# Taking the weight splitting off GpSimd: low parts on VectorE, high parts on ScalarE, from the last routing of a routed mixture-of-experts layer on

## The chip, the cores and the metric

The kernel runs on one core of a Trainium2 chip. The metric is the device time of one execution in microseconds (us). Engines are called as the profile calls them: PE (TensorE, matrix products), DVE (VectorE), ACT (ScalarE), POOL (GpSimd) and SP (SyncE, which issues most transfers). Each engine works through its own instructions in the order of the program; semaphores tie the engines together.

## The reference

Three stages follow each other: attention with rotary embedding, a dense mixture of four experts on all tokens, and a routed layer of eight experts in which each token goes to one expert. The last two stages, cut to their core:

```python
# dense: x [1152, 512], w1 [4, 512, 1024], w2 [4, 1024, 512]
for e in range(E):
    h = np.maximum(x @ w1[e], 0.0)
    out += p[:, e:e + 1] * (h @ w2[e])

# routed: 8 experts of the same size
logits = xn @ en.T / tau
expert_idx = np.argmax(logits, axis=1)
gate_w = probs[np.arange(N), expert_idx]
for e in range(E):
    mask = expert_idx == e
    h = np.maximum(x[mask] @ w1[e], 0.0)
    out[mask] = gate_w[mask, None] * (h @ w2[e])
```

Inputs and outputs are float32.

## The kernel before

**Precision.** PE multiplies in float32r. To keep float32 accuracy every operand is held as a high part and a low part, hi + lo, and a product is three matmuls: hi·hi, hi·lo, lo·hi. So all weights have to be split on the chip. A weight unit is a [128, 2048] piece of an expert's weights: units 0 and 1 are halves of w1, 2 and 3 halves of w2. It is loaded into `raw[u]` and split into `wh[u]` and `wl[u]` in four pieces j of [128, 512]: a copy makes the high part (`wh`), a subtraction raw - wh makes the low part (`wl`). There is one buffer of each kind per unit.

**Where the pieces are split.** In the dense layer ACT copies (L657) and DVE subtracts (L658). From the last routing on, POOL takes a share. For the first block of the routed layer `first_split` sends the low part to POOL unless the piece is named in `FIRST_ON_DVE`: 6 pieces on DVE, 10 on POOL. For all later blocks `split_piece` sends piece j = 3 of each unit to POOL, and for the odd units 1 and 3 the high part of that piece to DVE (L655) instead of ACT:

```python
def split_piece(self, u, j):
    self.split_rows(u, j, *([self.nc.gpsimd, self.nc.vector if u % 2 else None] if j == 3 else []))
```

**The last routing.** Tokens come in nine chunks of 128. Chunks 0 to 5 are routed together; the last three (6, 7, 8) are routed one by one by `route_one` as their sums of the dense layer end. The steps of one chunk are, in order: `finish` (x1 from the sums, L814, and its sum of squares, L894, both DVE; then the root on POOL, `norm`, L905 and L906), `turn` (PE transposes x1, ACT copies to `xt`, L889), up to three steps of weight splitting, `pick` (PE logits, L900; DVE maximum `lm`, one-hot `oh`, reciprocal of the root L1082, `nb` L1084; ACT exponential `ex`, L1085), the other steps of splitting, and `slots` (PE ranks, L919 to L921; DVE slot numbers and gate, L1090 to L1095). `scatter` (L928, an indirect transfer issued by POOL) sends x1 to its expert's rows. The products of the sums run on PE between these steps (L804 to L806). After chunk 8 DVE makes a table of blocks (`block_table`), whose last part SP reads for the control of the loads.

**The routed layer.** 14 blocks of 128 tokens are always there (`SURE`); three more are conditional. For block b, `fc1(b, u)` is 12 matmuls (L1291, tile psa) with unit u, `relu` an ACT activation (L1315, h), `turn_h` four PE transposes (L1268), an ACT copy `hth` (L1269) and a DVE subtraction `htl` (L1270); `turn_x` does the same for the input (`bxh`, `bxl`); `fc2(b, u)` is 12 matmuls (tile pso) with unit 2 + u. In `block(b)` the order on PE is: turn_x(b+1), fc1(b, 1), turn_h(b, 0), fc1(b+1, 0), turn_h(b, 1), fc2(b, 0), fc2(b, 1). Every block splits all four units, and one unit's four pieces are put out beside each of these four groups of 12 matmuls: unit 3 of b beside fc1(b, 1), unit 1 of b+1 beside fc1(b+1, 0), unit 0 of b+2 beside fc2(b, 0), unit 2 of b+1 beside fc2(b, 1). `finish` scales the result on ACT (L1326) and scatters it to the output (L1327, issued by POOL). The order of everything from the dense layer on is the order of the code; no planner moves it.

Of the kernel before, what the change touches and what calls it, by code (L numbers as in the profile page):

```python
# [28 lines left out]
class Schedule:  # L29
    """Puts operations of several engines in order: a greedy run over estimated costs, in which  # L30
    a free engine takes the operation of the lowest rank among those that can start by then."""
# [7 lines left out]
    def op(self, rank, eng, cost, f, *a, after=(), slot=None, late=0.0):  # L39
        """slot names a buffer of a ring, held from the first operation that names it until all  # L40
        in self.free[slot] are over; late is what the result takes beyond the engine's time."""
        o = dict(rank=rank, eng=eng, cost=cost, f=f, a=a, after=list(after), slot=slot, late=late, end=None)
        self.ops.append(o)
        return o

    def start(self, o, now):
        """When an operation can start, None as long as that is open."""
        ends = [now[o["eng"]], o["ready"]]
        if o["slot"]:
            used, n = self.used[o["slot"][0]], self.rings[o["slot"][0]]  # L50
            if o["slot"] not in used and len(used) >= n:
                for e in self.free[used[-n]]:
                    if e["end"] is None:
                        return None
                    ends.append(e["end"] + self.RELEASE)
        return max(ends)
# [5 lines left out]
    def run(self):  # L62
        """The operations, as dicts, by their start."""
# [32 lines left out]
class Attention:  # L96
    """RoPE attention, two heads at a time; x^T goes to xh + xl (both float32r).

    Round r runs the scores and the softmax of pair r beside the transposes and the
    products with v of pair r - 1, and prepares the operands of pair r + 1.  # L100
    """
# [36 lines left out]
    # engines of the operations that have a choice, pair by pair  # L138
# [58 lines left out]
    def rope(self, eng, i, j, sl=slice(0, 2), cols=slice(0, S)):  # L197
        """Step j of x * cos + swapped x * sin, in place; slot 0 is q, 1 is k."""
        raw = self.st[i]["raw"]
        x, y = raw[:, sl, cols], raw[:, slice(sl.start + 2, sl.stop + 2), cols]  # L200
        if j < 2:
            z = (x, y)[j]
            self.by(eng).tensor_tensor(out=z, in0=z, in1=self.rope_t[:, j, sl, cols], op=ALU.mult)
        else:
            self.by(eng).tensor_tensor(out=x, in0=x, in1=y, op=ALU.add)
# [11 lines left out]
    def spread(self, i):  # L217
        """qa = [qh; ql] of head A, qb = [ql; qh] of head B, ka and kb = k of a head on both halves."""
        nc, st, A, B = self.nc, self.st[i], self.A, self.B
        n = st["n"]  # L220
        ka = st["ka"] = self.p_k.tile([128, 2, S], F32R, name="ka")
        kb = st["kb"] = self.p_k.tile([128, 2, S], F32R, name="kb")
        qa, qb = st["qa"], st["qb"] = self.qa[i % 2], self.qb[i % 2]
        dma = lambda out, in_: nc.sync.dma_start(out=out.bitcast(F32), in_=in_.bitcast(F32))  # L224
        dma(out=ka[A], in_=n[A, 1:4:2])
        dma(out=ka[B], in_=n[A, 1:4:2])
        dma(out=qa[A, 0:S], in_=n[A, 0])
        dma(out=qa[B, 0:S], in_=n[A, 2])
        dma(out=kb[A], in_=n[B, 1:4:2])
        dma(out=kb[B], in_=n[B, 1:4:2])  # L230
        for o, m, f in ((0, 512, 0), (S, 64, 512)):
            dma(out=qb[A, o:o + m], in_=n[B, 2, f:f + m])
            dma(out=qb[B, o:o + m], in_=n[B, 0, f:f + m])

    def first_pair(self, D):
        """Loads and operands of pair 0, in small parts and without DMAs between partitions;
        what each chunk of its scores waits for."""
# [73 lines left out]
    def qk(self, i, c):  # L311
        """Scores of row chunk c; chunks 0-3 head A, 4 the rests of both, 5-8 head B."""
# [100 lines left out]
    def av(self, i, h, hf, k):  # L413
        """One of the five key chunks of x^T; any of them may come first."""
# [11 lines left out]
    def av_shift(self, i, h, hf):  # L426
        """The low half of x^T moves to the rows of the main half."""
# [51 lines left out]
    def plan(self, last_round):  # L479
        """All operations, with what they wait for."""  # L480
# [14 lines left out]
        for i in range(NPAIR):  # L495
            # operands
# [34 lines left out]
            # scores and softmax  # L531
# [15 lines left out]
            # transposes and products with v  # L547
# [57 lines left out]
class Experts:  # L605
    """Both expert layers. A weight unit is [128, 2048]: 0 and 1 are the halves of w1's columns
    as [p, k, 512], 2 and 3 the halves of w2's rows as [p, f, 512]; each is held as hi + lo."""
# [6 lines left out]
    FIRST_ON_DVE = (0, 0), (0, 1), (2, 0), (2, 1), (2, 2), (3, 0)  # L614
# [6 lines left out]
    def open_right(self, ctx):  # L621
        """Weights and the first split unit, in place of what the attention no longer needs."""
# [28 lines left out]
    def split(self, cut, u, lo_eng=None, hi_eng=None):  # L651
        nc = self.nc
        raw, hi, lo = cut(self.raw[u]), cut(self.wh[u]), cut(self.wl[u])
        if hi_eng:
            hi_eng.tensor_copy(hi, raw)  # L655
        else:
            nc.scalar.activation(out=hi, in_=raw, func=AF.Copy)  # L657
        (lo_eng or nc.vector).tensor_tensor(out=lo, in0=raw, in1=hi.bitcast(F32), op=ALU.subtract)  # L658

    def split_rows(self, u, j, *engines):  # L660
        self.split(lambda t: t[:, j * 512:(j + 1) * 512], u, *engines)

    def split_cols(self, u, j, *engines):
        self.split(lambda t: t.rearrange("p (a b) -> p a b", b=512)[:, :, j * 128:(j + 1) * 128], u, *engines)

# [18 lines left out]
    def layer1(self, xh, xl, rest):  # L684
        """All but the routing of the last token chunk, which is left in self.todo."""
        tc = self.tc
        with ExitStack() as c1:
# [28 lines left out]
            for c in range(3):  # L716
# [9 lines left out]
                # the first block's weights are split beside the chunk's routing  # L726
# [8 lines left out]
    def first_split(self, u, *js):  # L735
        for j in js:
            self.split_rows(u, j, *[] if (u, j) in self.FIRST_ON_DVE else [self.nc.gpsimd])

# [5 lines left out]
    def next_splits(self, n):  # L744
        """Splits of the weights needed next; a unit's next load follows its split."""
# [71 lines left out]

    def router_setup(self):
# [30 lines left out]
        def scale():  # L849
            """Embeddings over tau (|emb| + 1e-6)."""  # L850
# [11 lines left out]
        def empty():  # L862
            """Empty slots: zero rows whose token lies beyond the output."""
# [15 lines left out]
    def turn(self, c, cols, ps=None):  # L879
        """Part of a chunk's x1^T."""  # L880
# [27 lines left out]
    def counts(self, c, ps=None):  # L908
        """Tokens per expert in the chunks before c, in every partition."""
# [4 lines left out]
    def rank(self, cs):  # L914
        """Slots: the expert's region + tokens before in the chunk + tokens of the chunks before."""
# [8 lines left out]
    def scatter(self, c):  # L924
        # no order among the scatters can be declared between direct neighbours on the engine
# [7 lines left out]
    def route(self, chunks):  # L933
        """Logits and the one-hot of the first largest."""
# [7 lines left out]
        # the sums of the last token block leave half of the accumulators free  # L942
# [34 lines left out]
    def first_block(self):  # L977
        """The expert with the most tokens in the first six chunks comes first, the others follow in turn, and
        the slots of its first block are filled (or left empty) by these chunks alone, so that the second layer
        can start with that block. Then slots and gates of these chunks."""  # L980
# [5 lines left out]
        def choose():  # L986
# [8 lines left out]
            # e1 = the first expert, place = (e - e1) mod 8  # L995
# [9 lines left out]
            # 128 rows of NT / 128 place  # L1005
# [5 lines left out]
            # later tokens of the first expert start at slot 128  # L1011
# [36 lines left out]
    def first_loads(self, *units):  # L1048
        """The first expert's weights."""
# [4 lines left out]
    def route_one(self, c, acc, between):  # L1054
        """The whole routing of one chunk, from the last expert's sum on."""
# [45 lines left out]
    def apart(self, inst, group):  # L1101
        """Scatters to rows of their own need no order among themselves."""
# [4 lines left out]
    def block_table(self):  # L1107
        """For the blocks of the sorted tokens: whether the expert is new, its first unit, the first slot, and
        whether the block is there at all."""
# [5 lines left out]
        def rows():  # L1115
# [18 lines left out]
            # first slot: 128 j + sum over finished experts of (region - 128 blocks)  # L1134
# [116 lines left out]
    def split_with(self, b, u):  # L1251
        """The split of a unit, in pieces that go with the products that follow."""
# [4 lines left out]
    def split_piece(self, u, j):  # L1257
        self.split_rows(u, j, *([self.nc.gpsimd, self.nc.vector if u % 2 else None] if j == 3 else []))
# [29 lines left out]
    def three(self, acc, ah, al, u, first, last, mid=None, mid_at=1, low_last=False):  # L1288
        """acc += a^T w over the unit's four row chunks, without the product of the two low parts."""
# [43 lines left out]
def constants(nc, p):  # L1333
# [21 lines left out]
    # routing: strictly earlier rows, and tables over experts and blocks  # L1355
# [60 lines left out]
def rope_tables():  # L1416
    """cos and signed sin by (row d, table, position)."""
# [8 lines left out]
def weight_units(w1, w2):  # L1426
    """Per expert four contiguous units [128, 2048]: halves of w1's columns, halves of w2's rows."""
# [35 lines left out]
```

## Time and profile before

| | |
|---|---|
| median of 3 runs | 804.32 us (803.84 to 804.36) |
| span of the profiled execution | 802.5 us; the runs lie some 1.8 us above it |
| busy: PE, DVE, ACT, POOL | 749.2, 490.5, 377.1, 252.7 us |
| L658, low parts | DVE 222 pieces, 190.1 us; POOL 62 pieces, 105.2 us |
| L657, high parts on ACT | 258 pieces, 143.1 us |
| L655, high parts on DVE | 26 pieces, 10.8 us |
| mean granted clock of PE | 0.989 of 2.4 GHz |

The span is measured from the first to the last instruction; the time of a run lies around it. A busy time is the sum over an engine's instructions, so an instruction that stands still inside its own span also counts as busy. A start-to-start distance of two neighbours on an engine (here called pitch) is what an instruction costs the engine's queue; its own duration can be longer, because the end of one overlaps the start of the next.

The last routing lies at 582 to 618 us of the span, the first blocks at 618 to 644, and from 646.82 on ten rounds follow that look alike.

### The profile page before, as it was taken

The numbers are of one execution on the slowest core, as the hardware profiler recorded it, in microseconds if no ns is written. First come the engines' busy times: TensorE is split into PE (matmuls) and PEld (weight loads), VectorE is DVE, ScalarE is ACT, GpSimd is POOL, SyncE is SP. The second block draws the span as 40 slices with busy tenths as digits, with TensorE's granted clock in tenths as the row PEclk, the third lists the DMA queues.
The fourth block names the chain that finished last, engine by engine and source line by source line (L and its number), as shares of the span: only waits on it lengthen the run. The fifth ranks groups of instructions, "written<-read, shape, count | busy, mean of one in ns | idle before, by whom it ended". The sixth has DMA issues, their size and how long they took to land.

```text
span 802.5 us, 11114 instructions
## 1 busy us (share of the span) xinstructions
PE 749.2 (93%) x4002; PEld 653.4 (81%) x4002; DVE 490.5 (61%) x840; ACT 377.1 (47%) x767; POOL 252.7 (31%) x180
## 2 busy tenths in 40 slices
PE   2798888999999999999999999999988799999996
PEld 1687777889999999999999999999966577777775
DVE  7889999997122351222512225232558999999994
ACT  5587888884101231112311123111234788788883
POOL 4777685223100000000000000000084567665662
PEclk9899999999999999999999999999997999999999
DMA  6766664534340089900390000000071265594010
GB/s 200 218 168 162 170 162 89 142 131 185 139 124 0 1 239 313 288 1 1 130 291 0 1 1 1 0 1 1 21 292 43 93 230 206 187 376 155 27 41 17
DMA packets 31837, 97.27 MB, mean 121 GB/s; under 512 B 4638, under 2 KB 6174, under 8 KB 25760
## 3 DMA queue, kind: packets, MB, share of 16 engines
q1 hardware_dynamic: 29936, 91.77, 36.6%
q0 software_dynamic: 1840, 4.73, 1.6%
q8 instruction: 33, 0.54, 0.3%
q14 instruction: 28, 0.23, 0.1%
HBM read 58.32 MB, written 27.09 MB: 106 GB/s over the span
## 4 chain that ended last, share of the span: by engine, by line
PE 58%; DVE 23%; issue 7%; ACT 5%; POOL 3%; SPq 2%; DMA 2%; ACTq 0%; POOLq 0%; DVEq 0%
DVE wl L658 12%; PE ps L788 8%; PE ps L790 8%; PE ps L789 8%; PE acc L806 8%; PE acc L804 8%; PE acc L805 8%; PE av L424 2%; PE sc L327 2%; DVE nm L337 2%; SPq L224 2%; PE psa L1291 1%; ACT wh L657 1%; DVE p L411 1%; ACT e L344 1%
## 5 line engine op out<-in xcount | busy, mean ns | idle before, releaser
L794 DVE SCALAR_TENSOR_TENSOR hl<-ps,hh 128x384 fp32r<-128x384 f32 x96 | 53.5, 558 | 269.6 <-ACT hh L793 269.6
L658 DVE TENSOR_TENSOR wl<-raw,wh 128x512 fp32r<-128x512 f32 x222 | 190.1, 897 | 4.7 <-ACT wh L657 4.7
L793 ACT ACTIVATE hh<-ps 128x384 fp32r<-128x384 f32 x96 | 47.1, 491 | 304.5 <-PE ps L790 302.9
L657 ACT ACTIVATE wh<-raw 128x512 fp32r<-128x512 f32 x258 | 143.1, 627 | 5.2 <-DMA raw<-in_w_dram 2.8
L788 PE MATMUL ps<-xh,wh 128*128 128x384 f32 x384 | 130.3, 339 | 0.0
L790 PE MATMUL ps<-xh,wl 128*128 128x384 f32 x384 | 129.7, 338 | 0.0
L789 PE MATMUL ps<-xl,wh 128*128 128x384 f32 x384 | 129.5, 337 | 0.0
L658 POOL TENSOR_TENSOR wl<-raw,wh 128x512 fp32r<-128x512 f32 x62 | 105.2, 1714 | 49.4 <-DVE wh L655 27.3
L905 POOL TENSOR_TENSOR ss<-ss,half 128x1 f32<-128x1 f32 (+1 forms) x5 | 3.5, 704 | 355.1 <-DVE sq L894 355.1
L806 PE MATMUL acc<-wh,hl 128*128 128x512 f32 x288 | 114.4, 397 | 0.0
L804 PE MATMUL acc<-wh,hh 128*128 128x512 f32 x288 | 114.4, 397 | 0.0
L805 PE MATMUL acc<-wl,hh 128*128 128x512 f32 x288 | 113.7, 395 | 0.0
L789 PEld LDWEIGHTS ps<-xl,wh 128*128 128x128 f32 x384 | 72.2, 188 | 3.9
L788 PEld LDWEIGHTS ps<-xh,wh 128*128 128x128 f32 x384 | 72.2, 188 | 3.8
L790 PEld LDWEIGHTS ps<-xh,wl 128*128 128x128 f32 x384 | 72.1, 188 | 0.0
L806 PEld LDWEIGHTS acc<-wh,hl 128*128 128x128 f32 x288 | 54.2, 188 | 12.5
L805 PEld LDWEIGHTS acc<-wl,hh 128*128 128x128 f32 x288 | 54.2, 188 | 8.8
L804 PEld LDWEIGHTS acc<-wh,hh 128*128 128x128 f32 x288 | 54.1, 188 | 8.3
L344 ACT ACTIVATE e<-sc,nm 128x576 f32<-128x576 f32 x72 | 53.4, 742 | 9.7 <-DVE nm L337 9.4
L337 DVE TENSOR_REDUCE nm<-sc 128x1 f32<-128x576 f32 x72 | 53.8, 750 | 2.8 <-PE sc L327 1.7
L389 PE MATMUL pt<-ident,e 128*128 128x128 f32 (+1 forms) x304 | 47.6, 283 | 7.4 <-DVE ptl L411 6.3
L1291 PE MATMUL pso<-wh,htl 128*128 128x512 f32 x112 | 44.6, 407 | 5.0 <-DVE htl L1270 5.0
(233 smaller groups left out, 1298.9 us busy)
## 6 DMA issues: line engine op xcount, KB each, us to landing
raw<-in_w_dram SPq DMA_DIRECT2D x40, 1024.0 KB, 5.6
xs<-z SPq DMA_DIRECT2D x10, 2056.0 KB, 14.3
raw<-in_qk_dram SPq DMA_DIRECT2D x7, 1152.0 KB, 5.3
ka<-n SPq DMA_DIRECT2D x14, 288.0 KB, 3.9
kb<-n SPq DMA_DIRECT2D x14, 288.0 KB, 4.4
xin<-xs SPq DMA_DIRECT2D x13, 257.0 KB, 4.0
rv<-in_v_dram SPq DMA_DIRECT2D x8, 320.0 KB, 5.4
qa<-n SPq DMA_DIRECT2D x14, 144.0 KB, 4.2
```

Source lines behind the costliest of these rows:

```text
L337: nc.vector.tensor_reduce(out=st["nm"][:, c:c + 1], in_=st["sc", c][:, :, :SH], axis=AX.XY, op=ALU.max, negate=True)
L344: nc.scalar.activation(out=e.rearrange("p (a b) -> p a b", a=2), in_=st.pop(("sc", c))[:, :, :SH], func=AF.Exp, bias=st["nm"][:, c:c + 1], ...
L657: nc.scalar.activation(out=hi, in_=raw, func=AF.Copy)
L658: (lo_eng or nc.vector).tensor_tensor(out=lo, in0=raw, in1=hi.bitcast(F32), op=ALU.subtract)
L788: nc.tensor.matmul(o, wcut(self.wh[u], k), xh[:, k, cs], start=(k == 0), stop=False)
L789: nc.tensor.matmul(o, wcut(self.wh[u], k), xl[:, k, cs], start=False, stop=False)
L790: nc.tensor.matmul(o, wcut(self.wl[u], k), xh[:, k, cs], start=False, stop=(k == 3))
L794: nc.vector.scalar_tensor_tensor(out=hl, in0=o, scalar=0.0, in1=hh.bitcast(F32), op0=ALU.max, op1=ALU.subtract)
L804: nc.tensor.matmul(acc, hh[:, js], wh, start=(f == 0), stop=False)
L805: nc.tensor.matmul(acc, hh[:, js], wl, start=False, stop=False)
L806: nc.tensor.matmul(acc, hl[:, js], wh, start=False, stop=(f == 7))
L1291: self.nc.tensor.matmul(acc, a[:, k * 128:(k + 1) * 128], w[u][:, k * 512:(k + 1) * 512], start=start, stop=stop)
```

## The change

From the last routing on, every piece is split as in the dense layer: ACT copies the high part and DVE subtracts the low part. `FIRST_ON_DVE` and the choice of engines go. 62 subtractions move from POOL to DVE (10 in the routing, 52 in the blocks), and 26 copies from DVE to ACT. Nothing is computed otherwise. The rest of the diff takes out comments and docstrings, four code lines less in all, so a line of the kernel after has a number four lower than before from `first_split` on (L658 is L654).

```diff
-    FIRST_ON_DVE = (0, 0), (0, 1), (2, 0), (2, 1), (2, 2), (3, 0)
...
-    def split(self, cut, u, lo_eng=None, hi_eng=None):
+    def split(self, cut, u):
         nc = self.nc
         raw, hi, lo = cut(self.raw[u]), cut(self.wh[u]), cut(self.wl[u])
-        if hi_eng:
-            hi_eng.tensor_copy(hi, raw)
-        else:
-            nc.scalar.activation(out=hi, in_=raw, func=AF.Copy)
-        (lo_eng or nc.vector).tensor_tensor(out=lo, in0=raw, in1=hi.bitcast(F32), op=ALU.subtract)
+        nc.scalar.activation(out=hi, in_=raw, func=AF.Copy)
+        nc.vector.tensor_tensor(out=lo, in0=raw, in1=hi.bitcast(F32), op=ALU.subtract)
...
     def first_split(self, u, *js):
         for j in js:
-            self.split_rows(u, j, *[] if (u, j) in self.FIRST_ON_DVE else [self.nc.gpsimd])
+            self.split_rows(u, j)
...
     def split_piece(self, u, j):
-        self.split_rows(u, j, *([self.nc.gpsimd, self.nc.vector if u % 2 else None] if j == 3 else []))
+        self.split_rows(u, j)
```

The first place is DVE's queue in the routing of chunk 6, from `nb` of its `pick` to chunk 7's `finish` (acc_5137 holds chunk 7's sums; raw_2067, wh_2218 and wl_2219 are unit 1). Before:

```order
L1084 TENSOR_SCALAR nb<-lm_5169,ss 128x1
L1090 SCALAR_TENSOR_TENSOR rk_5198,sl_5199<-ps,oh 128x8
L1092 CAST slot<-sl_5199 128x1
L1093 TENSOR_SCALAR es_5178<-es_5178 128x1
L1094 RECIPROCAL x_2072<-es_5178 128x1
L1095 TENSOR_TENSOR seen<-seen,oh 128x8
L814 SCALAR_TENSOR_TENSOR x_2072<-acc_5137,p,x_2072 128x256 x2
L894 SCALAR_TENSOR_TENSOR sq,ss<-x_2072 128x512
L1077 TENSOR_REDUCE lm_5251<-ps 128x1
```

And in the changed kernel:

```order
L1080 TENSOR_SCALAR nb<-lm_5169,ss 128x1
L654 TENSOR_TENSOR wl_2219<-raw_2067,wh_2218 128x512 x3
L1086 SCALAR_TENSOR_TENSOR rk_5198,sl_5199<-ps,oh 128x8
L1088 CAST slot<-sl_5199 128x1
L1089 TENSOR_SCALAR es_5178<-es_5178 128x1
L1090 RECIPROCAL x_2072<-es_5178 128x1
L1091 TENSOR_TENSOR seen<-seen,oh 128x8
L810 SCALAR_TENSOR_TENSOR x_2072<-acc_5137,p,x_2072 128x256 x2
L890 SCALAR_TENSOR_TENSOR sq,ss<-x_2072 128x512
L654 TENSOR_TENSOR wl_2219<-raw_2067,wh_2218 128x512
L1073 TENSOR_REDUCE lm_5251<-ps 128x1
```

Three subtractions of unit 1 now stand between chunk 6's `nb` and its slots, ahead of chunk 7's `finish`, and a fourth ahead of chunk 7's `pick`; before, POOL had them.

The second place is DVE's queue in one of the later blocks, from `bxl` to the next `bxl` (units by their tiles: wl_2223 is unit 3, wl_2219 unit 1, wl_2071 unit 0, wl_2221 unit 2). Before:

```order
L1270 TENSOR_TENSOR bxl<-ps,bxh 128x512
L1280 CAST btok<-xin 128x1
L658 TENSOR_TENSOR wl_2223<-raw_2069,wh_2222 128x512
L655 CAST wh_2222<-raw_2069 128x512
L658 TENSOR_TENSOR wl_2223<-raw_2069,wh_2222 128x512 x2
L1270 TENSOR_TENSOR htl_5843<-ps,hth_5842 128x512
...
L658 TENSOR_TENSOR wl_2219<-raw_2067,wh_2218 128x512
L655 CAST wh_2218<-raw_2067 128x512
L658 TENSOR_TENSOR wl_2219<-raw_2067,wh_2218 128x512 x2
...
L1270 TENSOR_TENSOR htl_5877<-ps,hth_5876 128x512
L658 TENSOR_TENSOR wl_2071<-raw_2066,wh_2070 128x512 x3
```

And in the changed kernel:

```order
L1266 TENSOR_TENSOR bxl<-ps,bxh 128x512
...
L1276 CAST btok<-xin 128x1
L654 TENSOR_TENSOR wl_2223<-raw_2069,wh_2222 128x512 x4
L1266 TENSOR_TENSOR htl_5843<-ps,hth_5842 128x512
...
L654 TENSOR_TENSOR wl_2219<-raw_2067,wh_2218 128x512 x4
L1266 TENSOR_TENSOR htl_5877<-ps,hth_5876 128x512
...
L654 TENSOR_TENSOR wl_2071<-raw_2066,wh_2070 128x512 x4
L654 TENSOR_TENSOR wl_2221<-raw_2068,wh_2220 128x512
```

Each group of three subtractions (with a copy in it for units 3 and 1) has become four subtractions; the instructions between the groups stand where they stood.

## Rows read from the trace of the kernel before

**Rows 1.** Chain of work that ended last, 560 to 803 us: shares by line.

```profile
by line: DVE wl L658 39.1%; issue 16.6%; PE psa L1291 4.5%; ACT wh L657 4.5%; PE pso L1291 3.7%; DVE htl L1270 3.5%; POOL wl L658 3.0%; DVE wh L655 2.9%; POOL xs L928 2.7%; DVE bxl L1270 2.7%; PE ps L788 1.5%; PE ps L790 1.4%; PE ps L789 1.
```

**Rows 2.** Busy time by stretch: PE, PEld, DVE, ACT, POOL, clock, DMA share.

```profile
612.00:624.00 12.00, 11.95 (x46) 9.14 (x45) 9.54 (x32) 6.45 (x13) 3.55 (x3) 0.73 0.22 66
646.82:776.32 129.50, 126.86 (x602) 101.25 (x601) 129.50 (x181) 106.26 (x201) 84.62 (x50) 1.00 0.50 179
```

**Rows 3.** Line L658 over the span, by engine: nanoseconds min/median/max.

```profile
L658 DVE TENSOR_TENSOR wl<-raw,wh x222: 674/684/3199, 186.8 to 789.6; 128x512 fp32r<-128x512 f32 x111
...
L658 POOL TENSOR_TENSOR wl<-raw,wh x62: 1262/1729/2271, 591.4 to 789.2; 128x512 fp32r<-128x512 f32 x62
```

**Rows 4.** DVE in order of time in one round: start, duration in us.

```profile
647.42 0.14 DVE L1280 CAST btok<-xin 128x1 int32<-128x1 f32 x1
647.48 0.68 DVE L658 TENSOR_TENSOR wl<-raw,wh 128x512 fp32r<-128x512 f32 x1
648.08 0.41 DVE L655 CAST wh<-raw 128x512 fp32r<-128x512 f32 x1
648.42 1.28 DVE L658 TENSOR_TENSOR wl<-raw,wh 128x512 fp32r<-128x512 f32 x2
649.62 0.68 DVE L1270 TENSOR_TENSOR htl<-ps,hth 128x512 fp32r<-128x512 f32 x1
650.22 1.18 DVE L658 TENSOR_TENSOR wl<-raw,wh 128x512 fp32r<-128x512 f32 x1
```

**Rows 5.** ACT in order of time: eight copies of one round.

```profile
651.77 4.27 ACT L657 ACTIVATE wh<-raw 128x512 fp32r<-128x512 f32 x8
```

**Rows 6.** PE in order of time: the first three products of fc2(b, 1) in one round.

```profile
731.53 0.39 PE L1291 MATMUL pso<-wh,hth 128*128 128x512 f32 x1
...
731.76 0.39 PE L1291 MATMUL pso<-wl,hth 128*128 128x512 f32 x1
...
732.42 0.50 PE L1291 MATMUL pso<-wh,htl 128*128 128x512 f32 x1 [0.27 <-DVE htl L1270]
```

**Rows 7.** POOL in order of time in the last routing.

```profile
591.44 6.71 POOL L658 TENSOR_TENSOR wl<-raw,wh 128x512 fp32r<-128x512 f32 x5
...
608.13 2.51 POOL L658 TENSOR_TENSOR wl<-raw,wh 128x512 fp32r<-128x512 f32 x2
```

**Rows 8.** DVE in order of time, last routing and first blocks.

```profile
592.67 0.86 DVE L814 SCALAR_TENSOR_TENSOR x<-acc,p,x 128x256 f32<-128x256 f32 x2
...
596.33 0.17 DVE L1077 TENSOR_REDUCE lm<-ps 128x1 f32<-128x8 f32 x1 [1.80 <-PE ps L900]
...
599.03 0.16 DVE L1082 RECIPROCAL ss<-ss 128x1 f32<-128x1 f32 x1 [0.85 <-POOL ss L906]
...
608.00 3.20 DVE L658 TENSOR_TENSOR wl<-raw,wh 128x512 fp32r<-128x512 f32 x1 [0.26 <-ACT wh L657]
611.13 0.15 DVE L1077 TENSOR_REDUCE lm<-ps 128x1 f32<-128x8 f32 x1
...
636.67 0.68 DVE L1270 TENSOR_TENSOR htl<-ps,hth 128x512 fp32r<-128x512 f32 x1
```

**Rows 9.** ACT in order of time, last routing and first block.

```profile
592.19 1.66 ACT L657 ACTIVATE wh<-raw 128x512 fp32r<-128x512 f32 x3
...
619.98 2.19 ACT L657 ACTIVATE wh<-raw 128x512 fp32r<-128x512 f32 x4 [0.83 <-SPq L1242]
```

**Rows 10.** PE in order of time, last routing to last block.

```profile
593.20 0.89 PE L885 MATMUL ps<-ident,x 128*128 128x128 f32 x4 [0.22 <-DVE x L814]
...
612.05 0.17 PE L921 MATMUL ps<-oh,before 128*128 128x8 bf16 x1 [2.87 <-DVE oh L1081]
...
641.74 0.50 PE L1291 MATMUL pso<-wh,htl 128*128 128x512 f32 x1 [1.32 <-DVE htl L1270]
...
644.15 0.60 PE L1268 MATMUL ps<-ident,xin 128*128 128x128 f32 x4
...
792.03 0.50 PE L1291 MATMUL pso<-wh,htl 128*128 128x512 f32 x1 [0.55 <-DVE htl L1270]
```

More of the change, by code (lines that the diff above doesn't have):

```diff
@@ L649, in load1, with split_rows, split_cols @@
         self.nc.sync.dma_start(out=self.raw[u], in_=self.w1_d[e * 4 + u])
-    def split(self, cut, u, lo_eng=None, hi_eng=None):
+    def split(self, cut, u):
         nc = self.nc
         raw, hi, lo = cut(self.raw[u]), cut(self.wh[u]), cut(self.wl[u])
-        if hi_eng:
-            hi_eng.tensor_copy(hi, raw)
-        else:
-            nc.scalar.activation(out=hi, in_=raw, func=AF.Copy)
-        (lo_eng or nc.vector).tensor_tensor(out=lo, in0=raw, in1=hi.bitcast(F32), op=ALU.subtract)
[L660 to L664, printed above, removed]
+        nc.scalar.activation(out=hi, in_=raw, func=AF.Copy)
+        nc.vector.tensor_tensor(out=lo, in0=raw, in1=hi.bitcast(F32), op=ALU.subtract)
+    def split_rows(self, u, j):
+        self.split(lambda t: t[:, j * 512:(j + 1) * 512], u)
+    def split_cols(self, u, j):
+        self.split(lambda t: t.rearrange("p (a b) -> p a b", b=512)[:, :, j * 128:(j + 1) * 128], u)
     def open_layer1(self, ctx):
```

## Prediction, made blind

> **What bounds the kernel now.** I read the chain of work that ended last first: behind 560 us two fifths of it are DVE's subtractions, and PE's products of the routed layer are under a tenth [rows 1]. The change touches nothing ahead of 586 us, so the rest is read from that stretch, in three parts.
>
> The ten alike rounds (646.82 to 776.32 us): 12.95 us each, DVE busy for all of it, PE 12.69, ACT 10.63, POOL 8.46, clock 1.00 [rows 2]. One round in DVE's order of time gives the costs of its queue, start to start [rows 4]: btok 0.06, a copy L655 0.34 (648.08 to 648.42), two subtractions 1.20 (648.42 to 649.62), so 0.60 each, htl 0.60. By these a round of 12 subtractions, 2 copies, 3 of htl and bxl, and btok would take 7.20 + 0.68 + 1.80 + 0.06 = 9.74 us. It takes 12.95. The missing 3.21 us lie in the subtractions: the one at 650.22 shows 1.18 us, others up to 3.20, against a median of 0.684 [rows 3, 4]. At 608.00 one of them stands for 3.20 us while POOL does two from 608.13 to 610.64 [rows 7, 8]. So a piece that POOL subtracts costs DVE 3.21 / 4 = 0.80 us of standing still; a piece that DVE subtracts itself costs it 0.60.
>
> What PE loses in a round: the third product of fc2(b, 1) starts 0.66 us after the second, where 0.23 is the step before it, since htl is late behind DVE's subtractions [rows 6]. That is 0.43 us, and the other products follow each other without a gap, so PE alone would need 12.52 us a round.
>
> The last routing (582 to 618 us) is a chain of small DVE steps, and POOL's root of the squares stands in it. For chunk 7 that root waits behind five subtractions (591.44 to 598.15), and DVE's reciprocal gets it at 599.03 [rows 7, 8]. For chunk 8 the long subtraction at 608.00 holds `lm` until 611.13, and PE waits 2.87 us for the one-hot [rows 8, 10].
>
> **The change, part by part.** Rounds: DVE gives up 2 copies (0.68) and 3.21 us of standing still, and takes 4 subtractions (2.40): 12.95 - 0.68 - 3.21 + 2.40 = 11.46 us. ACT takes 2 copies at (4.27 - 0.63) / 7 = 0.52 start to start [rows 5]: at most 10.63 + 1.04 = 11.67 us. Both lie under PE's 12.52, which becomes the bound. Order within a round: in the 3.2 us of a group on PE, DVE has four subtractions (2.40) and one htl (0.60), so htl is done about 2 us before its product. Weights have still more room, since a unit is split right after its last use and wanted two groups later at the earliest. Gain: 0.43 us in each of the ten rounds and once more in block 12, which has the same wait: 11 × 0.43 = 4.7 us.
>
> The last block: the third product waits for htl at 792.03 [rows 10], which stood behind DVE's last contended subtractions. Four at 0.60 end before htl's ACT copy does, so its wait of 0.55 shrinks to that copy's: 0.5 us earlier.
>
> Last routing, chunk 6: DVE takes two more pieces (1.2 us of subtractions, some 0.8 past the old end). They are covered: its reciprocal waits for POOL's root anyway, which is late behind six scatters [rows 7]. POOL goes on to its subtractions, right behind that root, only at 591.44. Without that cover it would cost 0.8. Three pieces of unit 1 then stand between `nb` and the slots. Their copies start on ACT at 592.19, 0.52 apart [rows 9]; the third ends at 593.86, DVE's third subtraction ends its turn at 594.67, the five small slot steps take 0.7, and chunk 7's sums are taken at 595.36 instead of 592.67 [rows 8]: a loss of 2.7, for PE too, whose transposes wait at 593.20 [rows 10].
>
> Chunk 7: its `lm` moves by these 2.7 from 596.33 to 599.0 [rows 8]. The root is ready by then, POOL having nothing else, so the reciprocal follows four small steps later, at 599.8 instead of 599.03 [rows 8]: 0.8 of the loss is left. Chunk 8: two pieces at 0.60 in place of one that stood still beside POOL's next two turn this into a gain of 0.3. Then ACT's five copies, 0.52 apart from about 605.5, and five subtractions behind them end at 609.2, where `lm` starts instead of at 611.13 [rows 8]: 1.9 us gained. The last piece of unit 3 now stands ahead of the last part of the block table: 0.6 back. The control of the loads, and with it ACT's first copy for block 1 at 619.98 [rows 9], comes 1.3 us earlier.
>
> Blocks 1 and 2: from that copy to htl of block 1 at 636.67 DVE takes 16.7 us [rows 8, 9]. In that stretch stand, after the change, 20 copies on ACT and seven other activations of some 0.5: 20 × 0.52 + 3.5 = 13.9, and 0.6 more until htl starts: 14.5 us; DVE's own work, 22 × 0.60 and two of btok, is 13.3. So 2.1 us are gained. The wait of 1.32 at 641.74 for the next htl [rows 10] shrinks to some 0.3: 1.0. The transposes of block 3's input, at 644.15 [rows 10], so come 1.3 + 2.1 + 1.0 = 4.4 us earlier; I take 4.3, as a new load for unit 0 starts only when its buffer is free.
>
> Sum: 4.3 + 4.7 + 0.5 = 9.5 us. The profiled span of 802.5 becomes 793.0. The median of the runs lies 1.8 above the span: **794.8 us**.
>
> Bounds of what no row shows. A DVE subtraction in these stages with POOL silent costs between 0.60 [rows 4] and what it takes now, (12.95 - 2.54) / 12 = 0.87. I take 0.60, since 222 subtractions have a median duration of 0.684, those of the dense layer, where POOL does none, among them [rows 3]. A copy on ACT costs between 0.52 and its full 0.63 if none overlaps its neighbour; eight in a row show 0.52 [rows 5].
>
> **The rivals.** *The long subtractions are not POOL's doing* (transfers, ACT's copies, the semaphores): then each costs 0.87 after the change too, a round on DVE is 16 × 0.87 + 1.86 = 15.8 us, 2.8 more than now, and eleven of them make 31 us, the time 835 and slower. It decides from 0.69 us a subtraction on, where DVE's round reaches 12.95. Against it: two in 1.28 at 648.42, and the 3.20 beside POOL's two [rows 4, 7, 8]. Chance 0.04. The Trainium skill has a rule on this side ("Perfetto Trace Analysis", section "Optimizing Scalar/DVE Operations"): where DVE is saturated, work may be moved off it, even to GpSimd; by that, DVE at 129.50 of 129.50 us [rows 2] is the last engine to give work to. The same section warns that the two share a read port. Another page ("SBUF — State Buffer", section "Who interferes with whom") is sharper: a DVE instruction with two SBUF inputs and a GpSimd one that reads SBUF exclude each other for their whole length. By that each POOL piece could hold DVE for its whole 1.26 us [rows 3], a round of before would be up to 9.74 + 5.04 = 14.8 us, and the standing still would go with POOL's work. The trace shows it in kind and 0.80 in size.
>
> *ACT becomes the bound*: copies at 0.63 and the other activations' 3.3 (10.63 - 14 × 0.52) make 13.4 us a round, 0.45 more than now, 5 us in eleven, which eats the gain of the start: 804, no change. Against it: the eight copies in 4.27 [rows 5]. Chance 0.04.
>
> *A new wait takes the place of htl's*: with DVE and ACT both above nine tenths of a round and four subtractions ahead of each htl, the rounds stay at 12.95. Then only start and end gain: 804.3 - 4.8 = 799.5. Chance 0.10.
>
> *The start loses what it gains*: PE stands for 2 to 3 us at 593 to 596 for chunk 7's sums, and its clock may fall, as it did around the stalls of before (0.73 from 612 to 624, after the wait of 2.87) [rows 2, 10]. At half clock I estimate twice the step of 0.23 [rows 6]; six products stand between chunk 7's transposes and its logits, so 1.4 us go, and the logits themselves slow. With other small steps late, 2 to 4 of the 4.3 us are lost: 797 to 799. Chance 0.14.
>
> **How the numbers follow.** The forecast has 0.68; its own range is 792 to 797. A change within 0.2% (1.6 us) is about what a measurement of this kernel can't tell from none. The third and fourth rival end faster too, so faster has 0.68 + 0.10 + 0.14 = 0.92 less some doubt on all of them, 0.90; the same 0.04, slower 0.06. The range from 791.5 to 800 takes in all but the first two rivals and the doubt.
>
> **What will show it.** In the profile after: POOL without a subtraction; DVE's subtractions at 0.68 with hardly any above 0.75; rounds of 12.5 us in which PE has no wait over 0.1 and DVE idles for about 1 us; `lm` of chunk 7 late by 2.7 us and of chunk 8 early by 2. The prediction is wrong if subtractions stay long without POOL, if htl still holds PE, or if chunk 7's delay reaches the first block.

## The result, and the profile after

The changed kernel takes 791.75 us (median of four runs, 791.61 to 792.08); the kernel before took 804.16 on the same chip (four runs, 803.84 to 804.36). The ratio is 0.9845, with a 95% interval from 0.9833 to 0.9857: faster, since the interval lies wholly below 1. The time is 3 us better than the forecast of 794.8: inside the stated range of 791.5 to 800, but only just, and below the 792 to 797 that the prediction gives the forecast itself. By the profiled executions the span fell from 802.5 to 789.4 us, 13.1 us where 9.5 were forecast. The medians of the runs fell by 12.4: a run of the changed kernel lies 2.1 to 2.2 us above its span, not 1.8, which no run explains.

Where the 13.1 us came from. The marks between the parts are ACT's first copy for block 1 and PE's transposes of a block's input:

| part | forecast | measured | from which starts |
|---|---|---|---|
| routing, up to the first copy of block 1 | 1.3 | 2.4 | 619.98 [rows 9], now 617.59 |
| blocks 1 and 2, up to the transposes of block 3's input | 3.0 | 3.9 | 24.17 us [rows 9, 10], now 20.25 |
| ten rounds, up to the transposes of block 13's input | 4.3 | 5.7 | 129.53 us, now 123.85 |
| from there to the end | 0.9 | 1.1 | 28.82 us, now 27.71 |

First the busy times of the engines and the low parts (count, then nanoseconds min/median/max), from the page and from the view of line L654 (L658 before, [rows 3]) of the kernel after:

```profile
PE 743.1 (94%) x4002; PEld 651.9 (83%) x4002; DVE 471.2 (60%) x876; ACT 390.2 (49%) x793; POOL 145.3 (18%) x118
...
L654 DVE TENSOR_TENSOR wl<-raw,wh x284: 679/684/1352, 187.1 to 777.4; 128x512 fp32r<-128x512 f32 x142
```

All 284 low parts are DVE's, at the same median of 684 ns as before. DVE does 62 subtractions more and 26 copies less, and is busy for 19 us less (490.5 before): the long subtractions are gone.

The rounds, in busy time by stretch (the columns of [rows 2]): the end of the routing with block 0, then nine rounds from `bxl` to `bxl` of the kernel after.

```profile
612.00:624.00 12.00, 10.92 (x50) 7.79 (x50) 10.68 (x30) 8.62 (x17) 1.54 (x2) 1.00 0.33 95
...
651.62:763.11 111.49, 111.49 (x542) 91.77 (x541) 105.67 (x182) 104.74 (x199) 9.05 (x10) 1.00 0.50 182
```

A round is now 111.49 / 9 = 12.39 us instead of 12.95. PE is busy for all of it; DVE, which was, works 105.67 / 9 = 11.74 us, and ACT 11.64. (A busy time counts the overlap of two neighbours once, so it is less than the sum of their durations.) The bound has passed from DVE to PE, and PE's clock in 612 to 624 is 1.00 where it was 0.73.

One round in DVE's order of time, after (to be held against [rows 4]):

```profile
725.94 0.69 DVE L1266 TENSOR_TENSOR bxl<-ps,bxh 128x512 fp32r<-128x512 f32 x1 [0.51 <-ACT bxh L1265]
726.55 0.14 DVE L1276 CAST btok<-xin 128x1 int32<-128x1 f32 x1
726.61 2.49 DVE L654 TENSOR_TENSOR wl<-raw,wh 128x512 fp32r<-128x512 f32 x4
729.09 0.69 DVE L1266 TENSOR_TENSOR htl<-ps,hth 128x512 fp32r<-128x512 f32 x1
729.69 2.49 DVE L654 TENSOR_TENSOR wl<-raw,wh 128x512 fp32r<-128x512 f32 x4
...
732.93 4.90 DVE L654 TENSOR_TENSOR wl<-raw,wh 128x512 fp32r<-128x512 f32 x8
```

Four subtractions take 2.49 us, eight 4.90, so 0.60 each and none longer. DVE now waits for ACT's `bxh` in place of being waited for.

The same products as in [rows 6] in PE's order of time: the first of fc2(b, 1) in a round of the kernel before, with the product that follows the late one,

```profile
732.42 0.50 PE L1291 MATMUL pso<-wh,htl 128*128 128x512 f32 x1 [0.27 <-DVE htl L1270]
732.76 0.39 PE L1291 MATMUL pso<-wh,hth 128*128 128x512 f32 x1
...
773.68 0.60 PE L1268 MATMUL ps<-ident,xin 128*128 128x128 f32 x4
```

and PE after: chunk 7's transposes, chunk 8's ranks, block 1, block 3's and block 13's input, and the last block.

```profile
595.71 0.80 PE L881 MATMUL ps<-ident,x 128*128 128x128 f32 x4 [1.64 <-DVE x L810]
...
610.11 0.17 PE L917 MATMUL ps<-oh,before 128*128 128x8 bf16 x1 [1.19 <-DVE oh L1077]
...
632.43 0.50 PE L1287 MATMUL pso<-wh,htl 128*128 128x512 f32 x1 [0.56 <-DVE htl L1266]
...
635.06 0.39 PE L1287 MATMUL pso<-wl,hth 128*128 128x512 f32 x1
635.43 0.50 PE L1287 MATMUL pso<-wh,htl 128*128 128x512 f32 x1
...
637.84 0.60 PE L1264 MATMUL ps<-ident,xin 128*128 128x128 f32 x4
...
761.69 0.60 PE L1264 MATMUL ps<-ident,xin 128*128 128x128 f32 x4
...
778.57 0.40 PE L1287 MATMUL pso<-wl,hth 128*128 128x512 f32 x1
778.96 0.50 PE L1287 MATMUL pso<-wh,htl 128*128 128x512 f32 x1
```

Before, the late product itself took 0.34 us until the next one started (732.42 to 732.76), where 0.23 is the step between products that wait for nothing, so a stall of 0.43 cost PE 0.54. After, no product of the rounds waits, and in the last block the third product follows the second by 0.39 us instead of 0.94.

The last routing after, in DVE's order of time (for [rows 8]):

```profile
595.08 0.87 DVE L810 SCALAR_TENSOR_TENSOR x<-acc,p,x 128x256 f32<-128x256 f32 x2
...
598.73 0.17 DVE L1073 TENSOR_REDUCE lm<-ps 128x1 f32<-128x8 f32 x1 [0.55 <-PE ps L896]
...
599.53 0.16 DVE L1078 RECIPROCAL ss<-ss 128x1 f32<-128x1 f32 x1
...
609.17 0.16 DVE L1073 TENSOR_REDUCE lm<-ps 128x1 f32<-128x8 f32 x1
...
614.08 0.18 DVE L1137 SCALAR_TENSOR_TENSOR ctl<-blkno,row 128x17 int32<-128x17 f32 x1
614.18 0.68 DVE L1266 TENSOR_TENSOR htl<-ps,hth 128x512 fp32r<-128x512 f32 x1
614.78 0.68 DVE L654 TENSOR_TENSOR wl<-raw,wh 128x512 fp32r<-128x512 f32 x1
...
631.69 0.68 DVE L1266 TENSOR_TENSOR htl<-ps,hth 128x512 fp32r<-128x512 f32 x1
```

Chunk 7 loses and chunk 8 gains, each where the prediction put it. Chunk 6's sums, ahead of the change, come 0.27 us later in this execution (584.52 instead of 584.25), so the routing itself gains that much more than the times show. One row of the table of blocks had a size that the prediction missed; it is this one of the kernel before, in DVE's order of time:

```profile
616.24 1.01 DVE L1141 SCALAR_TENSOR_TENSOR ctl<-blkno,row 128x17 int32<-128x17 f32 x1
```

It writes 17 numbers a partition, yet it stood for 1.01 us, beside a subtraction that POOL had begun at 615.94; now it takes 0.18 (614.08). Chunk 7's `oh` shows the same: 1.19 us before (596.99), beside POOL's subtractions, and 0.23 now (599.39); there the wait for POOL's root hides it.

### The profile page after: what moved, and what is told of

Same layout as the page of the kernel before. It is cut to its first block, busy times and chain, and to the rows that moved or that the text cites. A ratio compares the mean times of both kernels' runs of the same rounds, so it can differ in the third digit from the quotient of the medians.

```text
span 789.4 us, 11018 instructions
## 1 busy us (share of the span) xinstructions
PE 743.1 (94%) x4002; PEld 651.9 (83%) x4002; DVE 471.2 (60%) x876; ACT 390.2 (49%) x793; POOL 145.3 (18%) x118
## 5 line engine op out<-in xcount | busy, mean ns | idle before, releaser
L654 DVE TENSOR_TENSOR wl<-raw,wh 128x512 fp32r<-128x512 f32 x284 | 178.6, 687 | 7.0 <-ACT wh L653 7.0
L653 ACT ACTIVATE wh<-raw 128x512 fp32r<-128x512 f32 x284 | 156.6, 627 | 4.1 <-SPq L1238 2.5
L327 PE MATMUL sc<-ka,qa 128*128 128x288 f32 x160 | 33.9, 333 | 17.0 <-POOL qa L187 14.7
L411 DVE TENSOR_TENSOR ptl<-pt,pth 128x512 fp32r<-128x512 f32 x68 | 45.7, 680 | 2.2 <-ACT pth L407 1.4
```

Source lines behind the costliest of these rows:

```text
L654: nc.vector.tensor_tensor(out=lo, in0=raw, in1=hi.bitcast(F32), op=ALU.subtract)
```

## The experiments

Every experiment is the changed kernel with the edit shown, timed against the kernel before on the same chip. The diffs are cut: where an engine is named in them, `split` and `split_rows` take engines again, as before.

**One part alone.** The changed blocks with the routing of before:

```diff
     def first_split(self, u, *js):
         for j in js:
-            self.split_rows(u, j)
+            self.split_rows(u, j, *[] if (u, j) in self.FIRST_ON_DVE else [self.nc.gpsimd])
```

> The change in the blocks alone; the first block's pieces are split as before (10 of 16 low parts on POOL). Theory: a piece that POOL subtracts makes DVE stand still for longer than DVE needs to subtract it, in every stage for itself. Then this kernel keeps the gain of the ten rounds (5.8 us between the traces of before and after), of the end (1.0) and of blocks 1 and 2 (3.9), and loses that of the routing (2.6): 804.2 - 10.7 = 793.5. Rival: the stages hang together (a late start is made up in the blocks, or an early one is lost there): 791.7 or over 796.

It took 794.48 us (ratio 0.9883, 0.9866 to 0.9899), with a span of 792.6. And the changed routing with the blocks of before:

```diff
     def split_piece(self, u, j):
-        self.split_rows(u, j)
+        self.split_rows(u, j, *([self.nc.gpsimd, self.nc.vector if u % 2 else None] if j == 3 else []))
```

> The change in the first block's pieces alone; the blocks send piece 3 of each unit to POOL and the odd units' high part to DVE, as before. Theory: 804.2 - 2.6 = 801.6, with rounds of 12.95 us as before and chunk 8's logits maximum at 609.2 of the span as in the kernel after. Rival, that the stages hang together: the two parts add up to more or less than the whole gain of 12.4 by over 1 us.

It took 802.2 us (0.998, 0.997 to 0.9989), with a span of 799.9. The rounds are 12.39 us in the first and 12.95 in the second: they follow from `split_piece` alone. By the spans the blocks give 9.9 us and the routing 2.6, together 12.5 of the 13.1. By the medians against the kernel before on the same chip they give 9.4 and 1.7, together 11.1 of the 12.4. So the parts fall short of the whole by 0.6 to 1.3 us, which the intervals of the two (1.3 and 0.8 us to either side) don't tell from nothing; whether the stages hang together within that is open. Both came within a microsecond of what was expected.

**Is it POOL that makes DVE's subtractions long, and by what?** Three kernels give POOL four operations a round on a 128x512 buffer of its own that nothing else reads or waits for; the weights stay with DVE and ACT, and the outputs are not touched. They differ in the operation alone:

```diff
     def split_piece(self, u, j):
         self.split_rows(u, j)
+        if j == 3:
+            z = self.idle[0]
+            self.nc.gpsimd.tensor_tensor(out=z, in0=z, in1=z, op=ALU.subtract)
```

(The lines that make the buffer are left out.) The second has a multiply by one there (`tensor_scalar`, one input), the third a `memset`, which reads nothing.

> As after, and POOL does one subtraction of 128x512 on a buffer of its own beside each unit's split, four a round, which nothing waits for (work added, none taken away). Theory, that POOL's reading makes DVE stand still: DVE's subtractions become long again, 3 us or more a round are lost, the rounds grow from 12.4 to 14.5 or more and the time to 815 or more. Rival, that the long subtractions of before came from waiting for POOL's results or from its place in the order: subtractions stay at 0.68 us, rounds at 12.4, time 792.

> The same with a multiplication by a number on POOL: one tensor read and one written. Theory: DVE stands still, for less than beside a subtraction since POOL reads half as much; rounds over 12.9, time over 797. Rival, that only two inputs on both sides collide: 792.

> The same with a memset of 128x512 on POOL in place of the subtraction: POOL writes and reads nothing. Theory, that it is reading that counts: no change, 792. Rival, that any POOL instruction on SBUF holds DVE: as with the subtraction, in proportion to its length.

The times are 832.09, 804.58 and 791.71 us, one run each, with rounds of 15.3, 13.2 and 12.4 us. DVE's subtractions from 650 to 770 us, by groups of instructions (count | busy us, mean ns | idle), in the changed kernel,

```profile
L654 DVE TENSOR_TENSOR wl<-raw,wh 128x512 fp32r<-128x512 f32 x155 | 95.7, 684 | 0.0
```

in the one with the routing changed alone, where POOL still subtracts real pieces,

```profile
L657 DVE TENSOR_TENSOR wl<-raw,wh 128x512 fp32r<-128x512 f32 x111 | 101.9, 962 | 0.0
...
L657 POOL TENSOR_TENSOR wl<-raw,wh 128x512 fp32r<-128x512 f32 x39 | 69.6, 1802 | 30.0 <-DVE wh L654 16.6 <-PE pso L1290 10.2 <-DMA raw<-in_w_dram 2.1
```

with POOL's idle subtraction,

```profile
L654 DVE TENSOR_TENSOR wl<-raw,wh 128x512 fp32r<-128x512 f32 x127 | 107.7, 910 | 0.0
...
L1259 POOL TENSOR_TENSOR idle<-idle 128x512 f32<-128x512 f32 x32 | 41.4, 1293 | 2.1
```

with its multiply,

```profile
L654 DVE TENSOR_TENSOR wl<-raw,wh 128x512 fp32r<-128x512 f32 x146 | 106.1, 789 | 0.0
...
L1259 POOL TENSOR_SCALAR idle<-idle 128x512 f32<-128x512 f32 x37 | 58.8, 1589 | 2.6
```

and with its memset:

```profile
L654 DVE TENSOR_TENSOR wl<-raw,wh 128x512 fp32r<-128x512 f32 x156 | 96.3, 684 | 0.0
...
L1259 POOL MEMSET idle<- 128x512 f32 x39 | 20.9, 535 | 1.7
```

The lengthening over 684 ns, times DVE's pieces, divided by POOL's, is what one POOL operation costs DVE: 278 ns × 111 / 39 = 0.79 us for a real piece, 226 × 127 / 32 = 0.90 for the idle subtraction, 105 × 146 / 37 = 0.41 for the multiply, nothing for the memset. The prediction's 0.80, taken from the length of a round, was right. Nobody waits for the idle buffer, so it is the work itself, not a semaphore. The cost doesn't go by how long POOL works (1.29, 1.59 and 0.54 us); it goes with what POOL reads: two inputs, one, none.

One meeting of the two in order of time shows how: in the kernel with the idle subtraction DVE's piece at 695.15 and POOL's at 695.26,

```profile
695.15 1.72 DVE L654 TENSOR_TENSOR wl<-raw,wh 128x512 fp32r<-128x512 f32 x1
```

```profile
695.26 1.05 POOL L1259 TENSOR_TENSOR idle<-idle 128x512 f32<-128x512 f32 x1
```

and in the kernel with the multiply, DVE's two pieces at 689.65 and POOL's at 689.54:

```profile
689.65 1.70 DVE L654 TENSOR_TENSOR wl<-raw,wh 128x512 fp32r<-128x512 f32 x2
```

```profile
689.54 1.54 POOL L1259 TENSOR_SCALAR idle<-idle 128x512 f32<-128x512 f32 x1
```

DVE's 1.72 is 1.04 over its 0.68, all of POOL's 1.05. Beside the multiply the two take 1.70 instead of 1.28, 0.42 of POOL's 1.54. The Trainium skill ("SBUF — State Buffer", section "Who interferes with whom") says that a VectorE instruction with two inputs in SBUF collides with a GpSimd instruction that reads SBUF, not with one that only writes, and that the loser stands still for the other's whole length. The memset's zero and the subtraction's 1.04 of 1.05 agree; the multiply's 0.42 of 1.54 does not, and there the measurement decides. Nor is it the whole length on the average of POOL's subtractions, 0.90 of 1.29 us.

**Does a round need its two copies on ACT?** The high part of piece 3 of the odd units goes back to DVE, its low part stays there, and POOL still splits nothing:

```diff
     def split_piece(self, u, j):
-        self.split_rows(u, j)
+        self.split_rows(u, j, None, self.nc.vector if j == 3 and u % 2 else None)
```

> As after, but the high part of piece 3 of units 1 and 3 stays on DVE (26 copies). Theory, that PE is now the bound: DVE's round grows by two copies of 0.34 us from 11.5 to 12.1 us, still under PE's 12.4, so the rounds stay at 12.4 and the time at 791.7 within 1 us. Rival, that the move of the copies to ACT carries part of the gain: each round up to 0.7 us longer, 797 to 799.

It took 793.69 us (0.9871, 0.9854 to 0.9887), 2 above the changed kernel, though the two intervals just overlap. The rounds are as expected, 12.41 us, but not by DVE's slack: a copy takes 0.46 us there, not 0.34, and DVE is busy for 111.1 of the 111.7 us of nine rounds. The loss lies in blocks 1 and 2, which was not expected. In PE's order of time there:

```profile
628.94 0.50 PE L1290 MATMUL psa<-wl,bxh 128*128 128x512 f32 x1 [0.83 <-DVE wl L657]
...
630.14 0.50 PE L1290 MATMUL psa<-wl,bxh 128*128 128x512 f32 x1 [0.24 <-DVE wl L657]
...
634.21 0.50 PE L1290 MATMUL pso<-wh,htl 128*128 128x512 f32 x1 [1.06 <-DVE htl L1269]
...
637.68 0.50 PE L1290 MATMUL pso<-wh,htl 128*128 128x512 f32 x1 [0.47 <-DVE htl L1269]
...
640.12 0.60 PE L1267 MATMUL ps<-ident,xin 128*128 128x128 f32 x4
```

PE waits 2.60 us for DVE here, in four places, where the changed kernel waits 0.56 (632.43) and 0.23 (628.82); block 3's transposes come at 640.12 instead of 637.84. That is 2.28 us later, and not all of it is the copies'. In this execution 0.2 are there at ACT's first copy for block 1 (617.79 instead of 617.59). PE's clock fell at 611.7 (last section), so its products for block 0 end later, ACT's `by` waits for them until 621.01 (620.16 in the changed kernel), and the copy that DVE's next group waits for comes later too:

```profile
622.25 0.69 DVE L657 TENSOR_TENSOR wl<-raw,wh 128x512 fp32r<-128x512 f32 x1 [0.63 <-ACT wh L656]
```

In the changed kernel that group starts at 621.39: 0.86 in all, 0.66 of it the clock's. From here on DVE has no slack: the weights of two blocks are split back to back, and in both kernels DVE works without a gap until block 3. Three copies at 0.46 us make the other 1.4. So the two copies of a round are worth next to nothing in the rounds, and the three in the first blocks 1.4 us.

**Is chunk 7's delay worth anything?** The prediction gives chunk 7 up to three pieces of unit 1 that stand ahead of its sums. Three kernels try to take that delay away. The first puts chunk 6's slots right behind its pick:

```diff
-        return [finish, idle, turn] + between[:3] + [pick] + between[3:] + [slots]
+        return [finish, idle, turn] + between[:3] + [pick, slots] + between[3:]
```

> As after, but in the routing of a chunk the slots come ahead of the second half of its splitting steps, so that chunk 6's three subtractions no longer stand ahead of chunk 7's sums. Theory: those sums are taken at about 592.6 instead of 595.1, PE's wait of 1.64 us for them goes, and 1 to 2 us of it reach the first copy for block 1: 790 to 790.7. Rival: what is gained for chunk 7 is lost again, since chunk 8's five copies on ACT and the loads behind them set its end: 791.7.

It took 794.78 us (0.9888, 0.9871 to 0.9904), 3 us slower than the changed kernel, and tells little on the question, since the edit does not do what was meant: the three pieces still stand ahead of the sums (593.02 to 594.84), and PE's ranks now stand ahead of six products that used to cover their wait. In PE's order of time:

```profile
610.44 0.17 PE L917 MATMUL ps<-oh,before 128*128 128x8 bf16 x1 [2.71 <-DVE oh L1077]
610.46 0.77 PE L1287 MATMUL psa<-wh,x0h 128*128 128x512 f32 x1
611.03 0.63 PE L1287 MATMUL psa<-wl,x0h 128*128 128x512 f32 x1
...
614.45 0.23 PE L907 MATMUL ps<-seen,ones 128*128 128x8 bf16 x1
```

After 2.71 us of standing still the products follow each other by 0.43 us instead of 0.23: PE has fallen to the lower of its two levels, 1.2 GHz (granted clock 0.89 in 600 to 612, 0.83 in 612 to 624, 1.00 in both in the changed kernel). And the count at 614.45, for which DVE's table of blocks waits, comes 3 us later than the changed kernel's. So the fall that the fourth rival feared after chunk 7's stall does happen in this kernel, here after a stall of chunk 8; in the changed kernel it did not, neither after chunk 7's 1.64 us nor after chunk 8's 1.19.

The second kernel gives the three pieces to POOL, the third leaves them on DVE but moves them behind chunk 7's sums (piece 3 of the unit, which stood there, falls behind chunk 7's maximum):

```diff
     def first_split(self, u, *js):
         for j in js:
-            self.split_rows(u, j)
+            self.split_rows(u, j, *[self.nc.gpsimd] if u == 1 and j < 3 else [])
```

> As after, but the low parts of pieces 0 to 2 of unit 1 in the routing go to POOL as before (3 of 62). They are the ones that stand ahead of chunk 7's sums on DVE. Theory: in this one place DVE has nothing to subtract beside them, so POOL holds up little; chunk 7's sums are taken at about 592.7, and 1 to 2 us are gained: 790 to 790.7. Rival: chunk 7's square root waits behind them on POOL, or DVE's sums stand still beside them: 791.7 or more.

```diff
-                between = [[(0, 0), (0, 3)], [(0, 1)], [(0, 2)], [(1, 0)], [(1, 1)], [(1, 2)]], [[(1, 3)]], [
+                between = [[(0, 0), (0, 3)], [(0, 1)], [(0, 2)]], [[(1, 0)], [(1, 1)], [(1, 2)], [(1, 3)]], [
```

> The changed kernel with three subtractions of unit 1, and their copies, moved in the code from chunk 6's routing to chunk 7's: they stand on DVE behind chunk 7's sums and squares and ahead of its maximum. POOL still splits nothing. If it is their place in DVE's queue that made chunk 7's sums late (595.08 in the changed kernel), the sums come at about 592.9 and the clock of PE holds: the time falls as in the run with the three pieces on POOL, to 790 to 791. If the delay only moves on, since the maximum of chunk 7 now waits for the three pieces (their copies start no earlier than about 591.5 and the maximum stood at 598.73), the time stays at 791.7 or above.

> The changed kernel once more, beside the run above on the same chip: 791.75 as measured first, within 0.4. The difference between the two says whether the place of three pieces is worth anything that can be told.

They took 790.39 us (0.9832, 0.9818 to 0.9846) and 790.92 (0.9837, 0.9824 to 0.985); the changed kernel, beside the third, 791.8 (0.9851, 0.9836 to 0.9866). The intervals overlap, so by the times alone neither is told from the changed kernel. The traces are finer. From chunk 6's sums to block 3's transposes the changed kernel takes 53.32 us in both of its profiled executions (584.52 to 637.84, 584.15 to 637.47), the one with three pieces on POOL 51.80 (584.72 to 636.52), the one with the later place 52.37 (585.71 to 638.08). Chunk 7's sums in these two, in DVE's order of time, three pieces on POOL,

```profile
592.89 0.88 DVE L813 SCALAR_TENSOR_TENSOR x<-acc,p,x 128x256 f32<-128x256 f32 x2
...
596.93 0.17 DVE L1076 TENSOR_REDUCE lm<-ps 128x1 f32<-128x8 f32 x1 [0.45 <-PE ps L899]
```

and with the later place:

```profile
593.89 0.88 DVE L810 SCALAR_TENSOR_TENSOR x<-acc,p,x 128x256 f32<-128x256 f32 x2
...
596.77 1.95 DVE L654 TENSOR_TENSOR wl<-raw,wh 128x512 fp32r<-128x512 f32 x3 [1.27 <-ACT wh L653]
598.65 0.15 DVE L1073 TENSOR_REDUCE lm<-ps 128x1 f32<-128x8 f32 x1
```

In both the sums come 8.2 us behind chunk 6's, in the changed kernel 10.6 (584.52 to 595.08). With the later place part of the delay only moves on to `lm`: it comes 12.9 us behind chunk 6's sums, 14.2 in the changed kernel, 12.2 with POOL. The same differences are there at ACT's first copy for block 1: 33.07 us behind chunk 6's sums in the changed kernel, 31.54 with POOL, 32.12 with the later place. So of the 1.5 us that POOL's three pieces save, some 1.0 is their place in DVE's queue, as far as one trace of each can tell.

## Why the prediction was right, and where it was short

**The rounds.** The step from 0.80 us of standing still for each POOL piece to a DVE round of 11.46 us holds: DVE is busy for 11.74, the standing still measured 0.79, and PE became the bound. The size was short: "PE alone would need 12.52 us a round" counted the 0.43 us by which the product came late, and not that this product itself takes 0.11 longer before the next one starts (732.42 to 732.76). With both the round is 12.95 - 0.54 = 12.41; measured 12.39. Ten rounds gave 5.7 us instead of 4.3. PE is now busy for the whole of a round, so the term that was mis-sized is PE's.

**The start.** Chunk 7's sums were forecast at 595.36 and came at 595.08; its `lm` at 599.0 and 598.73, its reciprocal at 599.8 and 599.53; chunk 8's `lm` at 609.2 and 609.17. Since chunk 6's sums came 0.27 later than before, the routing was 0.3 to 0.6 us quicker than forecast, and that the times meet so closely is in part luck. From there the prediction took 0.6 us back for the piece of unit 3 that now stands in the table of blocks. That piece is there (614.78) and costs its 0.6. What was left out is that the write of the control ahead of it stood still beside POOL too: from its start to the next instruction it took 0.93 us, and takes 0.10. The step that failed is the count of POOL's cost on subtractions alone; small instructions of DVE pay it as well. That is 0.8 of the 1.1 us between 1.3 and 2.4, and 0.2 are a shorter wait for PE's count. One of the prediction's signs of being wrong was that chunk 7's delay reaches the first block. On the whole it does not, since the first copy for block 1 comes 2.4 us earlier; but some 1.0 us of the delay is left there, as the kernel with the later place shows.

**Blocks 1 and 2.** From ACT's first copy to `htl` of block 1: 14.5 us forecast, 617.59 to 631.69 = 14.10 measured, so 2.6 gained where the prediction has 2.1 (its own 16.7 - 14.5 is 2.2). The size is near, but the step that gives it failed: ACT was to set the pace, with 13.9 us and 0.6 more until `htl` starts. ACT's `hth` ahead of that `htl`, in ACT's order of time after:

```profile
630.50 0.60 ACT L1265 ACTIVATE hth<-ps 128x512 fp32r<-128x512 f32 x1
```

It ends 13.5 us after the first copy, with six other activations instead of seven, and DVE takes `htl` 0.6 later. DVE sets the pace: it starts 0.66 us after ACT (618.25) and works on without a gap for 13.4 us, forecast as 13.3. That the two engines' sums lay so close together is why the time still came out. The wait of 1.32 us for the next `htl` was to shrink to 0.3; the product now follows the one before it by 0.37 us (635.06 to 635.43) instead of 1.70: 1.3 instead of 1.0. Together 3.9 us, where the prediction took 3.0.

**The end.** Forecast 0.5 for the last block and 0.43 for block 12; measured 0.55, and 0.56 in what remains of 1.1.

**The rivals.** That POOL is not the cause is refuted by the three kernels with idle work. The Trainium skill ("Perfetto Trace Analysis", section "Optimizing Scalar/DVE Operations"), on which that rival drew, lets a saturated VectorE hand work on even to GpSimd, and warns that the two share a port; here the warning decides, 0.79 us against 0.60. ACT as the bound and a new wait in place of `htl`'s would have shown as rounds of 12.95 or more. That the start loses what it gains did not happen: the clock held in both profiled executions of the changed kernel (1.00 from 588 to 640 us). Whether it must hold is open (below), so this rival was avoided with some luck.

Left open are the 0.6 to 1.3 us by which the two parts alone fall short of the whole. PE's granted clock in 612 to 624 is 0.86 in the kernel with the blocks alone, 0.93 in the one with the routing alone and 1.00 in the changed kernel, so part of it may be the clock; no run here shows how much.

## What to carry to other kernels

Where DVE's two-input operations show a long tail next to a tight median, look at what POOL does in the same microseconds: a piece handed to POOL here cost DVE 0.8 us of standing still against 0.6 for doing it itself, and DVE's busy time counted the standing still as work. Price such an offload by the length of a round, not by the share of busy time, and if POOL must work beside DVE, look first for work that reads little or nothing: the memset here cost DVE nothing. A queue's slack has to be read stage by stage: the copies that cost next to nothing in the rounds cost 1.4 us in the first two blocks.

## What the runs showed that was not expected

- POOL's multiply, with one input, takes longer than its subtraction with two (1.59 against 1.29 us on the average). That it costs DVE less was expected, and it is half (0.41 against 0.90 us); so the length of POOL's work says nothing of what it costs.
- A copy of a high part takes DVE 0.46 us from start to start in the kernel with two copies of a round back on DVE, and 0.34 in the one before [rows 4]; no run here explains it.
- A product that waited for its operand costs PE some 0.1 us more than the wait, at the full clock in every stall looked at (0.34 to the next product at 732.42 before, 0.33 at 632.43 after).
- PE's granted clock in 612 to 624 is 1.00 in the changed kernel and 0.86 in the one with two copies of a round back on DVE, although PE does the same in both until then, the wait of 1.19 us for `oh` just ahead included. In the second kernel PE stood at 1.2 GHz from about 611.7 (products 0.43 us apart), and was back at 2.4 GHz by 616 (0.23 apart); by block 2's transposes PE has made it up (624.05 against 623.83, and 0.20 lay between the two at 610.31 and 610.11 already), but it held up ACT and with it DVE by 0.66 us. So the clock's fall at such a place is not settled by the program alone.
